# A fused attention, max-of-three and normalised-layer kernel: operand loads, weight pieces, rounding order and tile pairs rearranged

## The chip, the cores and the metric

One core of one Trainium2 chip runs the whole kernel in one launch. The metric is device time of one execution in microseconds (us), median of the runs shown.

## The reference, cut to what matters

```python
scores = q @ k.T / sqrt(64) - log(448)             # 4 batches x 12 heads x 448 x 64
x = (1 / (1 + exp(-scores))) @ v                   # -> x: 1792 tokens x 768
h = max(x @ w1, x @ w2, x @ w3) @ w_out            # 768 -> 768 -> 768, no nonlinearity after w_out
h = h @ w_in                                       # 768 -> 1024
e = exp(h - max(h)); solu = h * e / (sum(e) + 1e-9)
ln = (solu - mean(solu)) / sqrt(var(solu) + 1e-6) * g_ln
out = ln @ moe2_w_out                              # 1024 -> 768
```

## The kernel before, in words

Every matmul is done with operands cut into a high part (the value rounded to the format that TensorE takes) and a low part (the value minus its high part). Three matmuls stand for one: high-high, high-low, low-high. The high part is a cast on ScalarE (ACT), the low part a subtraction on VectorE (DVE). Large products are taken seven at a time (P1 to P7 in `PROD`) with sums of blocks as operands (A11, S1 to S4, ... on one side, B11, T1 to T4, ... on the other).

The stages, in the order in which TensorE (PE) does them:

- First half of attention, 0 to about 95 us of the span.
- `gen_w` (L462): the product of `w_out` and `moe2_w_in`, which replaces two layers by one weight. Its parts go to DRAM tensors `w_d`. Between its matmuls `run_bg` (L328) takes steps of a queue `bg` of generators; in it stand `prepare` (operands of this product, tiles `r_wo`) and `convert_w2` (L406: one of 16 blocks of the last weight, scaled by `g`, cut and written to DRAM `w2_d`; tiles `raw`, `w2s`). Before, one block of the 16 stands there, two more in the second half of attention (150 to 216 us).
- The layer of w1, w2, w3 ("first layer"; `product`, L632): 9 groups of weights, each used by two units of 63 matmuls (token halves). `convert_group` (L557) prepares the next group in `bg`, and the remaining 13 blocks of `convert_w2` lie in the groups as `LATE` (L34) says. `RATE` (L36) is the number of steps for each matmul. `sums` (L650) gathers the result in tiles `hs` and writes them to DRAM `h_d` (L672).
- The bridge: `load_wf` (L714) brings seven weights of 1.5 MB from `w_d` through POOL's queue as the memory of the first layer comes free; `load_h` (L691) brings the tokens' `h` back from `h_d`, 128 tokens to a tile `a`, through SP's queue.
- Seven units "L" (each a pair of 128-token tiles, 63 matmuls of 512 columns), numbered L0 to L6, and then seven units "O" (84 matmuls of 384 columns), O0 to O6. `product_c` (L842) does one product; `prep_l` (L750) and `prep_o` (L946) prepare the seven operands of the next unit (tiles `c_L_A`, `c_L_S`, `c_O_A`, `c_O_S`), `solu_ln` (L879) normalises a tile of 128 tokens, transposes it and writes it to `u_d`, and `load_u` (L922) loads it as operand `ut`.

In the last 14 units the order of ACT's and DVE's instructions is written out by a credit. `pace` (L834) adds 0.227 (L) or 0.174 (O) after each matmul and, while the credit is positive, takes a step in turn from `bg` (operands) and `lazy` (normalising); each step states its cost. Before a product, `product_c` forces steps of `bg` until its operand has been issued:

```python
while key not in cops:
    assert step(bg), key
```

All instructions of PE, ACT and DVE run in that written order, each engine in its own queue. A unit runs P1, then P4 and P3 of the unit before it (`close`, L1006), then P2, P6, P5, P7. ACT copies the accumulator `X` out after P1 (L1038), P6 (L1073) and P7 (L1079) before PE may add the next product to it; DVE adds after P2, P7 and in `close`.

Of the kernel before, what the change touches and what calls it, by code (L numbers as in the profile page):

```python
# [6 lines left out]
F32 = mybir.dt.float32  # L7
# [25 lines left out]
EARLY, SECOND = 1, 2  # L33
LATE = (0, 1, 1, 2, 2, 2, 2, 2, 1)  # L34
RING = 10
RATE = (0.46, 0.38, 0.38) + 5 * (0.49,) + (0.4,)  # L36
# [9 lines left out]
def sigmoid_attention_max_moe_solu_ln(tc, q, k, v, w123, wo, wi, w2, g, out):  # L46
# [53 lines left out]
    w_d = {nm: dram.tile([P, 3, 2, 512], F32, name=f"w_d{nm}") for nm in LOADS}  # L100
# [8 lines left out]
    w2_second = w2_keys[EARLY : EARLY + SECOND]  # L109
    w2_left = [w2_keys[EARLY + SECOND + sum(LATE[:n]) : EARLY + SECOND + sum(LATE[: n + 1])] for n in range(NG)]  # L110
    rest_wo = [("wo", fc, i) for fc in range(1, FC) for i in range(2)]
    early = list(w2_keys[:EARLY])
    mid = rest_wo[:6]
    for n in range(6, len(rest_wo), 2):
        mid += [early.pop(0)] if early else []
        mid += [rest_wo[n], rest_wo[n + 1]]
    mid += early
    stream += mid + w2_second
# [56 lines left out]
    def prepare(key, fine=False):  # L175
        y = wip.tile([P, HU], F32, tag="y", name="y_" + "_".join(map(str, key)), bufs=3)
# [211 lines left out]
    sp.dma_start(out=g_sb, in_=g)  # L388
    MID = NP // 2
# [11 lines left out]

    FIN = [(nm, i) for i in range(3) for nm in TS]
    state["home"] = lambda k, name: stp.tile([P, 2 * QU], F32, tag="stg", name=name, bufs=2)
    state["w2s"] = 0

    def convert_w2(key):  # L406
# [17 lines left out]
        for n, src in enumerate((y[:, QU:], z[:, :QU], z[:, QU:], y[:, :OU])):  # L424
# [11 lines left out]
            (sp if state["home"] else pool).dma_start(  # L436
# [4 lines left out]
    def staging(name):  # L441
        k = state["w2s"]
        state["w2s"] += 1
        if k % 2 == 0 or state["home"] is None:
            return stp.tile([P, 2 * QU], F32, tag="stg", name=name, bufs=2)
        return state["home"](k, name)
# [15 lines left out]
    def gen_w(fc, n):  # L462
# [23 lines left out]
        def put(nm, src):  # L486
            t = wsp.tile([P, 2, 512], F32R, tag="ws", name=f"ws{nm}_{c}", bufs=3)
            copy(act, t[:, 0], src)
            yield
            rest(dve, t[:, 1], src, t[:, 0])  # L490
            sp.dma_start(out=w_d[nm][:, c], in_=t.bitcast(F32))
            yield
# [14 lines left out]
        if fc == FC - 1 and n == 0:  # L507
            wts[4] = temp(4)
            copy(act, wts[4], ps)
            bg.appendleft(put("B21", wts[4]))  # L510
        elif n == 1:
            b21 = pws[fc][:, 0] if fc < FC - 1 else wts[4]
            wts[2] = temp(2)
            tt(wts[2], ps, wts[1], ALU.subtract)
            tt(wts[3], ps, wts[3], ALU.subtract)
            now(put("B22", ps))
            if fc < FC - 1:
                now(put("B21", b21))
            tt(wts[1], b21, wts[2], ALU.subtract)
            bg.extendleft(put(nm, wts[k]) for nm, k in (("T4", 1), ("T3", 3), ("T2", 2)))  # L520

    wts = {}
    bg.extend(prepare(key, True) if key[0] == "wo" else convert_w2(key) for key in mid)
# [14 lines left out]
    state["home"] = None  # L538
# [58 lines left out]

    tsplits = [split_t(0, nm, i) for nm in ("T1", "T4", "T3", "T2") for i in range(3)]
    bg.append(mix(run_steps(tsplits + [convert_group(0)]), run_steps(convert_w2(key) for key in w2_second)))


# [89 lines left out]
    def load_h(p, k):  # L691

        for i in range(2):
            t = tiles[2 * p + i]
            a = f_tile(*FIN[4 * (1 - p % 2) + i + 2 * k], f"a{p}_{i}{k}")[:, :HU]
            sp.dma_start(
                out=a.rearrange("p (f t) -> p f t", f=3),
                in_=h_d[k][:, :, t * P : (t + 1) * P].rearrange("f p t -> p f t"),
            )
            hts[(p, i, k)] = a  # L700
# [38 lines left out]
    def split_l(key, src):  # L739
        t = place(key)  # L740
        while t is None:
            yield None
            t = place(key)
        copy(act, t[:, 0], src)
        yield 0.05
        rest(dve, t[:, 1], src, t[:, 0])
        cops[key] = [t[:, m] for m in range(2)]
        yield 0.56

    def prep_l(p):  # L750
        a11, a12, a21, a22 = (hts.pop((p, i, k)) for i, k in ((0, 0), (0, 1), (1, 0), (1, 1)))
        yield from split_l(("L", p, "A11"), a11)
        yield from split_l(("L", p, "A12"), a12)
        s1 = f_tile(*FIN[8 + p % 2], f"s1_{p}")[:, :HU]
        tt(s1, a21, a22, ALU.add)
        yield 0.56
        tt(a21, a11, a21, ALU.subtract)
        yield 0.56
        tt(a11, s1, a11, ALU.subtract)
        yield 0.56  # L760
        yield from split_l(("L", p, "S2"), a11)
        yield from split_l(("L", p, "S1"), s1)
        yield from split_l(("L", p, "S3"), a21)
        yield from split_l(("L", p, "A22"), a22)
        tt(a12, a12, a11, ALU.subtract)
        yield 0.56
        yield from split_l(("L", p, "S4"), a12)
# [3 lines left out]
    for n, u in enumerate(units):  # L771
# [8 lines left out]
        if old is not None:  # L780
# [4 lines left out]
            if old["u"] == (NG - 1, 1):  # L785
# [6 lines left out]
                load_h(0, 1)  # L792
# [11 lines left out]
        if u == (NG - 1, 1):  # L804
            loads = pin(ET.Pool)
            shut(xd_cm)
            wslot.update(weight_slots("sa", (0, 1)))
            for tag in (0, 1):
                load_wf(LOADS[tag], tag)
            load_h(0, 0)  # L810
# [56 lines left out]
    def new_st(t):  # L867
        st = tp.tile([P, 12], F32, tag="st", name=f"st{t}", bufs=16)
        return [st[:, i : i + 1] for i in range(12)]

    h2s, sts, uts = {}, {}, {}

    def add_max(dst, ps, other, top):
# [274 lines left out]
```

## Time and profile before

| | us |
|---|---|
| median of 3 runs | 815.06 (809.72 to 815.38) |
| the profiled execution | 810.48 |
| its span in the profile | 808.7 |
| PE busy / DVE busy / ACT busy in it | 684.3 / 501.6 / 376.1 |

The rows below come from one profiled execution. [...] An instruction's idle time is that of its engine just before it, with what ended it.

### The profile page before, as it was taken

The page shows a single profiled execution, that of the slowest core. Times are in us where ns is not written, and L with a number is a line of the kernel's source. Part 1 is how long each engine was busy: PE and PEld are TensorE (multiplying, and loading weights), DVE is VectorE, ACT ScalarE, POOL GpSimd, SP SyncE. Part 2 cuts the span into 40 slices and gives each one's busy share as a digit, 9 for nine tenths or more (in the row PEclk, how much of TensorE's full clock was granted, in tenths as well). Part 3 has the DMA queues.
Part 4 walks back from the last instruction along what each step waited for, and adds up shares of the span by engine and source line. Part 5 has one row for each costly group of instructions (what it writes and reads, how often), then busy time and mean ns, then how long its engine had stood idle before and what let it go on. Part 6 is the DMA issues. An engine that isn't in the chain of part 4 may idle for free.

```text
span 808.7 us, 9695 instructions
## 1 busy us (share of the span) xinstructions
PE 684.3 (85%) x3283; PEld 543.8 (67%) x3283; DVE 501.6 (62%) x1140; ACT 376.1 (46%) x716; POOL 73.4 (9%) x128
## 2 busy tenths in 40 slices
PE   9999979899999999999998256977776677767677
PEld 6555856445599999999998245755554577656567
DVE  3999866787587776887783225754454645454524
ACT  6886324678654445455540113643342443434322
POOL 1111110021000111101101010000014200000000
PEclk9999989899999999999999587998999978998869
DMA  8787577556113565466627692222157922313131
GB/s 292 215 258 236 186 263 278 189 177 174 64 35 99 154 201 151 120 193 203 168 54 278 243 324 59 86 85 65 39 145 249 273 84 92 98 62 101 59 94 60
DMA packets 79234, 125.43 MB, mean 155 GB/s; under 512 B 31984, under 2 KB 60048, under 8 KB 78288
## 3 DMA queue, kind: packets, MB, share of 16 engines
q1 hardware_dynamic: 68144, 69.72, 27.4%
q0 software_dynamic: 10896, 54.86, 21.3%
q8 instruction: 26, 0.43, 0.2%
q10 hardware_dynamic: 144, 0.23, 0.1%
q14 instruction: 24, 0.20, 0.1%
HBM read 84.41 MB, written 40.37 MB: 154 GB/s over the span
## 4 chain that ended last, share of the span: by engine, by line
PE 63%; DVE 16%; ACT 9%; DMA 8%; issue 3%; SPq 0%; ACTq 0%; DVEq 0%
PE x L642 15%; PE X L852 15%; PE v L642 7%; PE av L279 7%; PE V L852 5%; PE sc L258 5%; PE z L642 4%; DMA h_d<-hs 3%; DMA a<-h_d 2%; PE sc L254 2%; PE Z L852 2%; DVE h L886 1%; ACT c_O_S L52 1%; DVE h L874 1%; DMA w_dB<-wsB 1%
## 5 line engine op out<-in xcount | busy, mean ns | idle before, releaser
L279 PE MATMUL av<-sf,vr 128*64 128x448 f32 x384 | 79.8, 559 | 0.0
L266 ACT ACTIVATE sf<-sc,bias_s 128x896 f32<-128x896 f32 x72 | 67.8, 1010 | 1.5
L475 PE MATMUL pw<-wi_t,r_wo 128*128 128x512 f32 x216 | 53.1, 407 | 7.1 <-DVE r_wo L54 7.1
L258 PE MATMUL sc<-qt,kt 64*128 64x448 f32 x432 | 51.9, 379 | 4.8 <-ACT sf L263 4.7
L852 PE MATMUL X<-wfT,c_L_S 128*128 128x512 f32 x126 | 33.8, 413 | 26.0 <-ACT h L1073 16.6
L279 PEld LDWEIGHTS av<-sf,vr 128*64 128x64 f32 x384 | 26.0, 140 | 42.8 <-issue 37.1
L475 PEld LDWEIGHTS pw<-wi_t,r_wo 128*128 128x128 f32 x216 | 42.2, 197 | 18.1 <-DVE r_wo L54 7.9
L852 PE MATMUL X<-w2tT,c_O_S 128*128 128x384 f32 x168 | 38.2, 374 | 15.0 <-ACT c_O_S L52 13.6
L642 PE MATMUL x<-T3h,S 128*128 128x448 f32 x108 | 34.9, 378 | 17.5 <-ACT u L682 17.5
L258 PEld LDWEIGHTS sc<-qt,kt 64*128 64x128 f32 x432 | 39.0, 186 | 15.8 <-ACT sf L263 6.2
L148 POOL DMA_DIRECT2D raw<-in_w x52 | 28.4, 546 | 226.4 <-DVE w2s L57 122.6
L852 PE MATMUL X<-w2tB,c_O_A 128*128 128x384 f32 x84 | 27.4, 493 | 25.2 <-ACT c_O_A L52 24.4
L852 PEld LDWEIGHTS X<-wfT,c_L_S 128*128 128x128 f32 x126 | 23.7, 196 | 34.9 <-ACT h L1073 17.4
L852 PEld LDWEIGHTS X<-w2tT,c_O_S 128*128 128x128 f32 x168 | 32.2, 209 | 19.5 <-ACT c_O_S L52 15.9
L57 DVE TENSOR_TENSOR c_L_A<-a,c_L_A 128x384 fp32r<-128x384 f32 x21 | 11.6, 554 | 51.6 <-ACT c_L_A L52 51.6
L852 PEld LDWEIGHTS X<-w2tB,c_O_A 128*128 128x128 f32 x84 | 21.8, 282 | 29.8 <-ACT c_O_A L52 26.7
L682 ACT COPY u<-x 128x448 f32<-128x448 f32 x36 | 19.1, 531 | 47.3 <-PE x L642 47.2
L642 PEld LDWEIGHTS x<-T3h,S 128*128 128x128 f32 x108 | 21.1, 195 | 19.6 <-ACT u L682 17.8
L642 PE MATMUL x<-B11h,A 128*128 128x448 f32 x108 | 33.7, 366 | 0.0
L642 PE MATMUL v<-T1h,S 128*128 128x448 f32 x108 | 33.6, 365 | 0.0
L642 PE MATMUL v<-B22h,S 128*128 128x448 f32 x108 | 33.6, 365 | 0.0
L642 PE MATMUL x<-T2h,S 128*128 128x448 f32 x108 | 33.6, 365 | 0.0
(183 smaller groups left out, 1635.8 us busy)
## 6 DMA issues: line engine op xcount, KB each, us to landing
raw<-in_w POOLq DMA_DIRECT2D x52, 384.0 KB, 4.1
w_d<-w2s SPq DMA_DIRECT2D x42, 192.0 KB, 2.4
u_d<-ub SPq DMA_DIRECT2D x14, 512.0 KB, 2.7
ut<-u_d SPq DMA_DIRECT2D x56, 128.0 KB, 3.4
kr<-in_k SPq DMA_DIRECT2D x24, 256.0 KB, 3.6
vr<-in_v SPq DMA_DIRECT2D x24, 256.0 KB, 3.8
raw<-in_wi POOLq DMA_DIRECT2D x16, 384.0 KB, 4.5
w_dT<-wsT SPq DMA_DIRECT2D x12, 512.0 KB, 3.5
```

The costliest lines, as they stand in the source:

```text
L52: act.copy(dst, src)
L57: eng.tensor_tensor(out=dst, in0=src, in1=hi.bitcast(F32), op=ALU.subtract)
L148: pool.dma_start(out=t, in_=source(key).rearrange("p (n t) -> p n t", t=2))
L254: pe.matmul(sc[:, 0, :S], lhsT=kt[:, x, c * P :], rhs=qt[:, y], start=start, stop=stop)
L258: pe.matmul(sc[:, j, :S], lhsT=kt[rows, x, c * P : (c + 1) * P], rhs=qt[rows, y], start=start, stop=stop)
L266: act.activation(sf, sc[:, :, :S], AF.Sigmoid, bias=bias_s, scale=1.0 / math.sqrt(D))
L279: pe.matmul(pa[j * D : (j + 1) * D, :S], lhsT=vr[:, j, c], rhs=sf if c == 3 else sf[:, j], start=(n == 0), stop=(n == 3),)
L475: pe.matmul(ps, lhsT=wt[:, a, cols], rhs=wi_t[:, b, c0 : c0 + 512], start=(i == 0), stop=(i == 3 * KC - 1))
L642: pe.matmul(ps, lhsT=l, rhs=r, start=(start and c == 0 and i == 0), stop=(stop and c == 2 and i == 2), skip_group_check=True)
L682: act.copy(e, ps)
L852: pe.matmul(ps, lhsT=hl[l][:, c * P : (c + 1) * P], rhs=wt[:, c, m], start=(start and c == 0 and i == 0), stop=(stop and c == chunks - 1 a ...
L874: dve.tensor_tensor_reduce(out=dst, in0=ps, in1=other, scale=1.0, scalar=-3.0e38, op0=ALU.add, op1=ALU.max, accum_out=top)
```

## The change

- `convert_w2` leaves the `gen_w` stage and the second half of attention: all 16 blocks lie in the first layer, two in each of groups 1 to 8. The rates of groups 1 and 2 rise to that of the others. `ws` gets four buffers, `y` two.
- The weights in `w_d` get a row pitch of 528 instead of 512 numbers, so that a load of 1.5 MB consists of pieces of 2 KB instead of 12 KB.
- The first pair's `h` gets tiles of its own. Its first two thirds are loaded before the last sums, and its last third straight from `hs`.
- `prep` replaces `split_l` and `split_o`: the cast of the next operand is issued before the subtraction of the last, in 12 steps instead of 18. It is queued after P6 instead of before P2 (L) and after P2 (O).
- `load_u` stands before P2 instead of after it, and waits until the pair after it has been normalised too. `load_w2` for the last layer's first weight moves by one unit.
- `solu_ln` works on a pair of tiles: sign and 1/1024 are folded into other instructions, the one-column instructions work on two columns, and the transposed tile takes the memory of `e`.

```diff
-LATE = (0, 1, 1, 2, 2, 2, 2, 2, 1)
+LATE = (0,) + 8 * (2,)
-RATE = (0.46, 0.38, 0.38) + 5 * (0.49,) + (0.4,)
+RATE = (0.46,) + 7 * (0.49,) + (0.4,)
...
-    w_d = {nm: dram.tile([P, 3, 2, 512], F32, name=f"w_d{nm}") for nm in LOADS}
+    w_d = {nm: dram.tile([P, 3, 2, 528], F32, name=f"w_d{nm}") for nm in LOADS}
...
-    bg.extend(prepare(key, True) if key[0] == "wo" else convert_w2(key) for key in mid)
+    bg.extend(prepare(key, True) for key in rest_wo)
...
+    def last_rows(k):
+        for i in range(2):
+            t = tiles[i]
+            b, c0 = divmod(t * P, S)
+            sp.dma_start(out=hts[(0, i, k)][:, 2 * P :], in_=hs[(k, b)][:, c0 : c0 + P])
...
-        pool.dma_start(out=t.bitcast(F32), in_=w_d[nm])
+        pool.dma_start(out=t.bitcast(F32), in_=w_d[nm][:, :, :, :512])
...
+    def prep(kind, p, a11, a12, a21, a22, s1, view, cost):
+        ready = {}
+        def high(nm, src):
+            parts = halves_of((kind, p, nm))
+            while parts is None:
+                yield None
+                parts = halves_of((kind, p, nm))
+            ready[nm] = (src, parts)
+            copy(act, view(parts[0]), src)
+        def low(nm):
+            src, parts = ready.pop(nm)
+            rest(dve, view(parts[1]), src, view(parts[0]))
+            cops[(kind, p, nm)] = parts
+        yield from high("A11", a11)
+        yield 0.1
+        yield from high("A12", a12)
+        low("A11")
+        yield cost
+        tt(s1, a21, a22, ALU.add)
+        yield cost
+        low("A12")
+        yield cost
+        tt(a21, a11, a21, ALU.subtract)
+        yield cost
+        tt(a11, s1, a11, ALU.subtract)
+        yield cost
+        yield from high("S2", a11)
+        tt(a12, a12, a11, ALU.subtract)
+        yield cost
+        yield from high("S1", s1)
+        low("S2")
+        yield cost
+        yield from high("S3", a21)
+        low("S1")
+        yield cost
...
     def load_u(p):
         for t in tiles[2 * p : 2 * p + 2]:
-            while t not in turned:
+            while t not in turned or (p + 1 < NP2 and tiles[2 * p + 3] not in turned and p > 0):
                 assert step(lazy), t
...
         if n + 1 < NP2:
             load_h(p + 1, 0)
             load_h(p + 1, 1)
-            bg.append(prep_l(p + 1))
+        elif n + 1 < len(stage):
+            load_u(n + 1 - NP2)
...
-        if NP2 - 1 <= n < len(stage) - 1:
-            load_u(n + 1 - NP2)
-            bg.append(prep_o(n + 1 - NP2))
         product_c(X, kind, p, "P6", False, False)
         release(kind, p, "P6")
+        if n + 1 < NP2:
+            bg.append(prep_l(p + 1))
+        elif n + 1 < len(stage):
+            bg.append(prep_o(n + 1 - NP2))
```

The steps of `solu_ln` cost 0.2, 1.6, 0.3, 0.2, 0.7 and 1.25 for each tile before, 8.5 in 12 steps for a pair, and 7.64 in 13 steps after. `prep` costs 0.56 (L) or 0.69 (O) in each of 11 steps and 0.1 in one; before, an operand took 0.05 and 0.56 or 0.69 in two steps, and each of the four sums as much in one.

## Rows read from the trace of the kernel before

**Rows 1.** Stages of core 0: length, each engine's busy time and instructions, PEclk, DMA.

```profile
105.00:150.00 45.00, 35.12 (x153) 25.10 (x153) 28.50 (x58) 19.31 (x33) 2.69 (x5) 0.88 0.73 257
150.00:216.00 66.00, 63.97 (x384) 32.81 (x382) 47.43 (x108) 50.84 (x82) 9.13 (x14) 0.98 0.51 152
...
293.00:420.00 127.00, 127.00 (x628) 117.69 (x627) 99.80 (x238) 65.99 (x159) 14.04 (x26) 1.00 0.55 158
...
442.00:492.00 50.00, 16.56 (x67) 13.69 (x66) 12.93 (x25) 7.84 (x16) 3.21 (x6) 0.72 0.70 262
...
509.00:623.00 114.00, 84.35 (x319) 62.53 (x317) 60.81 (x166) 47.63 (x92) 9.99 (x14) 0.93 0.36 110
623.00:783.00 160.00, 116.28 (x498) 103.00 (x498) 77.26 (x172) 60.03 (x113) 7.13 (x10) 0.85 0.37 115
```

**Rows 2.** TensorE's timeline, 85 to 225: start, length, operation, count, idle before.

```profile
116.42 13.29 PE L475 MATMUL pw<-wi_t,r_wo 128*128 128x512 f32 x45 [5.93 <-DVE r_wo L54]
...
146.96 1.49 PE L258 MATMUL sc<-qt,kt 64*128 64x448 f32 x6 [2.78 <-ACT sf L263]
...
182.02 0.86 PE L258 MATMUL sc<-qt,kt 64*128 64x448 f32 x6 [1.89 <-ACT sf L263]
```

**Rows 3.** ScalarE's timeline, 88 to 118 us.

```profile
110.61 0.54 ACT L52 CAST w2s<-raw 128x192 fp32r<-128x192 f32 x2 [4.53 <-DMA w_d<-w2s]
```

**Rows 4.** TensorE's timeline, the bridge.

```profile
459.93 0.74 PE L642 MATMUL x<-T3h,S 128*128 128x448 f32 x1 [17.46 <-ACT u L682]
...
491.64 3.65 PE L852 MATMUL X<-wfT,c_L_S 128*128 128x512 f32 x9 [15.98 <-ACT h L1073]
```

**Rows 5.** ScalarE's timeline, the same stretch.

```profile
458.93 0.51 ACT L52 CAST c_L_A<-a 128x384 fp32r<-128x384 f32 x1 [24.60 <-DMA a<-h_d]
...
487.26 0.51 ACT L52 CAST c_L_A<-a 128x384 fp32r<-128x384 f32 x1 [17.31 <-DMA a<-h_d]
```

**Rows 6.** POOL's queue, 405 to 500 us.

```profile
431.93 1.08 POOL L716 DMA_DIRECT2D wfB<-w_dB  x2 [19.92 <-DMA a<-h_d]
```

**Rows 7.** DMA queues, 438 to 442 us: packets, MB, share of 16 engines.

```profile
q0 software_dynamic: 134, 1.49, 87.4%
q1 hardware_dynamic: 123, 0.20, 13.0%
```

**Rows 8.** DMA issues, 442 to 446 us: KB each, median us to landing.

```profile
h_d<-hs SPq DMA_DIRECT2D x2, 224.0 KB, 12.9
```

**Rows 9.** DMA queues, 612 to 616 us.

```profile
q0 software_dynamic: 336, 1.18, 89.4%
```

**Rows 10.** TensorE's timeline, first products of L1, L2 and O0.

```profile
495.13 2.20 PE L852 MATMUL X<-wfB,c_L_A 128*128 128x512 f32 x9
...
509.41 2.20 PE L852 MATMUL X<-wfB,c_L_A 128*128 128x512 f32 x9
...
622.98 3.88 PE L852 MATMUL X<-w2tB,c_O_A 128*128 128x384 f32 x12 [2.94 <-ACT c_O_A L52]
```

**Rows 11.** TensorE's timeline, waits of O3, first products of O3, O4, O6.

```profile
698.28 0.62 PE L852 MATMUL X<-w2tB,c_O_A 128*128 128x384 f32 x2 [3.94 <-ACT c_O_A L52]
...
710.83 2.73 PE L852 MATMUL X<-w2tT,c_O_S 128*128 128x384 f32 x12 [1.90 <-ACT c_O_S L52]
714.65 2.74 PE L852 MATMUL V<-w2tT,c_O_S 128*128 128x384 f32 x12 [1.09 <-ACT c_O_S L52]
...
723.55 3.84 PE L852 MATMUL X<-w2tB,c_O_A 128*128 128x384 f32 x12 [4.08 <-ACT c_O_A L52]
...
783.22 0.62 PE L852 MATMUL X<-w2tB,c_O_A 128*128 128x384 f32 x2 [3.58 <-ACT c_O_A L52]
```

**Rows 12.** Groups by line and form, 510 to 809 us, VectorE and ScalarE.

```profile
L57 DVE TENSOR_TENSOR c_O_A<-ut,c_O_A 128x512 fp32r<-128x512 f32 x21 | 14.4, 687 | 29.7 <-ACT c_O_A L52 29.7
...
L60 DVE TENSOR_TENSOR u<-V,u 128x384 f32<-128x384 f32 x14 | 7.8, 557 | 30.0 <-ACT u L1079 18.7 <-PE V L852 11.2
...
L1079 ACT COPY u<-X 128x384 f32<-128x384 f32 x7 | 3.3, 469 | 16.6 <-PE X L852 16.6
```

More of the change, by code (lines that the diff above doesn't have):

```diff
@@ L737, in place, with halves_of @@
         return ring.tile([P, 2, HU], F32R, tag="ring", name="c_" + "_".join(map(str, key)))
[L739 to L742, printed above, removed]
+    def halves_of(key):
+        if key[0] == "L":
             t = place(key)
[L744 to L748, printed above, removed]
+            return t if t is None else [t[:, m] for m in range(2)]
+        if not clear(state["ops"] - RING) or not clear(state["ops"] + 1 - RING):
+            return None
+        return [place(key).rearrange("p a b -> p (a b)")[:, :512] for m in range(2)]
@@ new lines, in prep @@
+    def prep(kind, p, a11, a12, a21, a22, s1, view, cost):
[33 more added lines that the diff above has]
+        yield cost
+        yield from high("A22", a22)
+        low("S3")
+        yield cost
+        yield from high("S4", a12)
+        low("A22")
+        yield cost
+        low("S4")
+        yield cost
@@ L865, in charge, with new_st, add_min @@
         credit["t"] -= cost
-    def new_st(t):
-        st = tp.tile([P, 12], F32, tag="st", name=f"st{t}", bufs=16)
-        return [st[:, i : i + 1] for i in range(12)]
     h2s, sts, uts = {}, {}, {}
-    def add_max(dst, ps, other, top):
+    turned = set()
+    def new_st(p):
+        st = tp.tile([P, 9, 2], F32, tag="st", name=f"st{p}", bufs=8)
+        sts[p] = [st[:, i] for i in range(9)]
+        return sts[p]
+    def add_min(dst, ps, other, low, first):
         dve.tensor_tensor_reduce(
-            out=dst, in0=ps, in1=other, scale=1.0, scalar=-3.0e38, op0=ALU.add, op1=ALU.max, accum_out=top
+            out=dst, in0=ps, in1=other, scale=-1.0, scalar=first, op0=ALU.add, op1=ALU.min, accum_out=low
@@ L1012, in close @@
         if kind == "L":
+            first, low = (x[:, 1:] for x in sts[p][:2])
             dve.tensor_scalar(
-                out=cx, in0=o["X"], scalar1=1.0, scalar2=None, op0=ALU.mult, op1=ALU.max, accum_out=o["top"][3]
+                out=cx, in0=o["X"], scalar1=-1.0, scalar2=first, op0=ALU.mult, op1=ALU.min, accum_out=low
             )
-            charge(0.85)
+            charge(0.78)
         else:
@@ L1022, in close @@
         if kind == "L":
-            add_max(u2, o["V"], u2, o["top"][1])
-            lazy.append(both(*(solu_ln(t) for t in tiles[2 * p : 2 * p + 2])))
+            first, low = (x[:, :1] for x in sts[p][:2])
+            add_min(u2, o["V"], u2, low, first)
+            lazy.append(solu_ln(p))
         else:
```

221 lines of the change are left out of this document (91 added, 130 removed).

## The prediction

> **What bounds the kernel now.** I read the stages first, then what TensorE waited for in each, then what stood ahead of that work in the other engines' queues. In the stages [rows 1] look at the first number after the length: from 293 to 420 us PE is busy all 127 us, so nothing done there for the other engines can show. It has no work in 9.9 of 45 us (105 to 150), 33.4 of 50 (442 to 492), 29.7 of 114 (509 to 623) and 43.7 of 160 (623 to 783). In none of these is DVE or ACT full: in the last stage they are busy 48% and 38%. So the last two stages are bound by the order of three in-order queues that wait for each other, not by an engine.
>
> The bridge has two holes, 17.46 and 15.98 us [rows 4]. PE's releaser there is ACT copying an accumulator; ACT itself had sat before an earlier instruction of its queue, a cast whose source `a` came by DMA, for 24.60 and 17.31 us [rows 5]. So the accumulator copy was stuck behind a late load. What made the load late: POOL started the weight loads at 431.93 [rows 6], and in the 4 us that follow 438 the software queue moved 134 packets of 1.49 MB (11 to 12 KB each) while SP's queue moved 123 packets of 0.20 MB [rows 7]. The two queues take turns packet by packet, so a small row pays for a 12 KB piece. A write of 224 KB took 12.9 us there [rows 8].
>
> Where one product follows another without a wait, an L unit takes 509.41 - 495.13 = 14.28 us for 63 matmuls, 0.227 each [rows 10]; that was L1, with the queue of normalising only beginning to fill. Later units are slower: L2 to O0 took 622.98 - 509.41 = 113.6 us for five units, and O3 723.55 - 698.28 = 25.3 us [rows 10, 11]. In O3 PE waits 1.90 us before P6, 1.09 before P5 and 4.08 before the next P1, 7.1 in all [rows 11]; 84 matmuls at the pace of 0.174 that `pace` assumes are 14.6 us, which leaves 3.6 for the granted clock, 0.85 on average in this stage [rows 1].
>
> **Blocks of the last weight.** One block leaves `gen_w`. ACT stood there 4.53 us for a DMA out of `w2s` [rows 3]; the operand cast behind it reached PE 5.93 us late, and the 45 matmuls after that took 13.29 us where 45 x 0.227 = 10.2 [rows 2]. Both go: 5.93 + 3.1 = 9.0. The waits at 146.96 and 182.02, 2.78 and 1.89 us [rows 2], are on ACT too; the second has the other two blocks beside it, of the first I cannot say what share is theirs. I take 11 of 13.7; between 4 (DVE, busy 63% there, is next late) and 14. The three blocks go to groups 1 and 2 and the last group. Their cover is a full PE: with two blocks in each group DVE is busy 99.8 of 127 us and PE never waits [rows 1]. A block is some nine DVE instructions; at 99.8 / 238 = 0.42 us each, 3.8 us, so three cost nothing there, and at most 11 if that cover failed. In the last group, 28 steps at 0.4 a matmul are 70 of its 126 matmuls, done before the bridge. Their writes join SP's queue ahead of the first `h` loads, which then have about 10 us until they are needed.
>
> **The bridge.** P7 of the last first-layer unit could have run at 459.93 - 17.46 = 442.5 [rows 4]. From there: P7 1.8 us, P1 of L0 2.0, the two left products 3.7, the other four of L0 8.2, all of L1 14.3: P1 of L2 at 472.5 instead of 509.41, 36.9 us earlier, if nothing waits. The first pair's operands no longer stand behind the weights: two thirds of each are loaded before, and the last third is a quarter of a megabyte in all, out of memory on the core. The second pair's load still follows the last writes of `h`, since it takes the memory of `hs`; I leave 1.5 us for it. What is late next is the weights, 11.0 MB in seven loads through one queue from 431.93. In 12 KB pieces they move at 1.49 MB in 87.4% of 4 us, 426 GB/s [rows 7]. No row shows 2 KB pieces of this queue; the nearest are its 3.5 KB packets, 1.18 MB in 89.4% of 4 us, 330 GB/s [rows 9], and as the average of those 4 us 295. I take 330. Then the first five (7.86 MB) are there at 456, when P7 of L0 wants the fifth, and the seventh at 466, when P3 of L0 wants it at 462: about 4 late. 36.9 - 1.5 - 4.4 = 31. At 426 the wait is gone (37); at 250, a guess below the last average for 2 KB and for the operand loads' turns, the seventh comes at 476, which leaves 20.
>
> [...]
>
> **The last twelve units.** The cause of their waits is the lead with which operands are issued. Before, the operands of an O unit are 18 steps (7 x 0.74 + 4 x 0.69 = 7.9) and the normalising of a pair 12 steps (8.5). A unit's credit is 14.6 less three charges of 0.56, 12.9. As the two queues take turns, 12.9 / (0.44 + 0.71) = 11 steps of each are taken: 7 of the 18 are left until a product forces them, that is, until they stand in ACT's and DVE's queues behind the copy and the sum that wait for PE's last product. Every operand is then a round trip. After: 12 steps of 0.64 against 13 of 0.59, so 12.9 / 1.23 = 10.5 of 12 are taken in time, and only one or two are forced. By the same sum an L unit goes from 10 of 18 to 10 of 12. By the order of the steps, those forced are the low parts of A11 (for P1) and of S2 (for P6); S1 for P5 comes ahead of the copy, so its 1.09 goes. What a forced P1 still waits for: the copy after P7, 0.47, the sum, 0.56, and one subtraction, 0.69 [rows 12], with hand-overs 1.9, less the two matmuls that need no low part, 0.35: 1.6. P6 likewise, with a sum of two operands in the place of the copy, 1.6. An O unit is then 14.6 + 3.2 + 1.7 for the clock (half of before's 3.6, as half of the waits are left) = 19.5; an L unit, with a shorter subtraction and a longer sum, 14.3 + 2.8 + 1.4 = 18.5. The normalising is paced to end at about O4 (`load_u` forces it there); O5 without it I put at 16, and O6 with the end at 24 instead of 808.7 - 783.22 = 25.5 [rows 11]. Sum 5 x 18.5 + 5 x 19.5 + 16 + 24 = 230 us instead of 808.7 - 509.41 = 299.3: 69 less. Bounds: 30 (rival two) and 105 (rival one).
>
> What these edits add: `load_u` now waits for one more normalised pair, and forces its steps ahead of P2; its eight DMAs go out ahead of the write of `e`. With `ub` in the memory of `e`, the second exponential of the next pair waits for a DMA out of the tile three back; behind it on ACT stand the casts and copies. In the credit's order the transpose lies some 4 us ahead of it, about the time of that write, so I put it at nothing, with one or two us for each of seven pairs as the worst. The 14 or so one-column instructions that fall away for each pair are taken from a DVE that is 48% busy: nothing by themselves.
>
> **Sum.** The profiled execution took 810.48 (span 808.7 and 1.8 around it): 810.5 - 11 - 31 - 69 = 699.5. The median of the runs stands 0.6% above that execution; half of that makes 701.
>
> **Rivals.** One, the lead suffices (chance 0.13): with integer steps nothing is forced, waits vanish as in L1. Twelve units at 15.3 to 16 and the end at 23 make 194, 105 less, and the whole 664. For it: L1 at 14.28 [rows 10]. Against: 10.5 is below 12. Two, ACT takes the place of the forced steps (0.2): its exponentials, squares and scalings wait for DVE in the middle of the queue, and copies stand behind them. Then little but the wait before P5 and some clock comes back, 30 us, and the whole is 738. For it: ACT already sits 30 us before DVE's sums can run [rows 12]. Three, a piece is not a turn (0.1): the operand loads stay at about 10 us in the bridge, and the second hole stays for the most part; 16 instead of 31 and the whole about 715. Against it: the one-to-one packets [rows 7]. [...] Four, slower (0.05): the 2 KB pieces cost POOL's software queue time for each piece. Seven loads have six times the pieces. The forecast turns into a loss when the seventh load lands 115 us later than 466, at 581: 21 us a load instead of 4. At six times the present pace, 3.7 us for 1.57 MB at 426 GB/s, it is 22 us a load and the whole about 820. Against it: the pieces of 3.5 KB already run at 330 [rows 9].
>
> **How the numbers follow.** The forecast, 701, has 0.52. From 670 to 742 lie it, the third and nearly all of the second; left out are most of the first and the fourth. Faster by over 1% (about what this kernel's runs can tell from no change) 0.95, within 1% 0.01, slower 0.04.
>
> **What would show it.** In the profile after: no hole above 3 us between 442 and 480 less 11; SP's packets landing in 3 to 4 us beside the weights; no r_wo wait of 6 us in `gen_w`; PE full through the first layer; O units of 19 to 20 us with no wait before P5 and waits of 1.5 to 2 before P1 and P6. It is wrong if the units still take 23 us and more, if ACT sits before `e` or `h` while PE waits for a copy, or if weights arrive after their products.

## The result, and the profile after

The changed kernel takes 713.25 us (median of 4 runs, 712.01 to 716.61); the kernel before, timed beside it, 813.49. The ratio is 0.8779, 95% interval 0.8732 to 0.8827. The forecast was 701. The profiled execution took 716.61 (the slowest of the four), its span 714.8 against 808.7: 93.9 us less, which I split where the prediction did; by the medians it is 100.2. The medians here and below leave out one slow execution, of 720.56 us, in one of the experiments.

The stages of the changed kernel (columns as in [rows 1]; times from the span's start, PEclk the clock granted to TensorE as a share of full speed). The whole first layer is one row, since the three blocks went to groups outside of 293 to 420. 430 to 488 goes from P7 of the last first-layer unit to P1 of L2 (442 to 509 before), 488 to 571 is L2 to L6 (509 to 623 before), 571 to 623 is O0 and O1, 623 to 715 is O2 to the end:

```profile
105.00:150.00 45.00, 41.51 (x215) 28.07 (x213) 34.09 (x67) 22.29 (x35) 1.61 (x3) 1.00 0.76 263
...
205.37:430.12 224.75, 224.75 (x1109) 207.74 (x1107) 174.78 (x407) 113.64 (x272) 24.86 (x45) 1.00 0.53 154
...
430.00:488.00 58.00, 37.64 (x135) 30.15 (x135) 22.49 (x45) 16.35 (x32) 6.34 (x9) 0.76 0.75 254
488.00:571.00 83.00, 76.19 (x320) 58.86 (x318) 61.55 (x142) 51.58 (x100) 5.70 (x8) 1.00 0.39 120
571.00:623.00 52.00, 39.23 (x164) 32.90 (x162) 24.34 (x45) 18.30 (x35) 11.41 (x16) 0.84 0.77 227
623.00:715.00 92.00, 82.15 (x444) 79.55 (x442) 51.86 (x92) 40.12 (x77) 0.00 (x0) 0.96 0.35 113
```

Look at PE's number and at the clock behind the POOL column. From 105 to 150 PE is busy 41.5 us instead of 35.1; the first layer is full with the three blocks in it and takes 224.8 us, where it took 224.6 before (217.85 to 442.47); five L units have few holes and the full clock. Two stages are still bad: 430 to 488 (37.6 busy of 58, clock 0.76) and 571 to 623 (39.2 of 52, clock 0.84).

**Until the bridge.** P7 of the last first-layer unit could have run at 441.76 - 11.64 = 430.1 instead of 442.5: 12.4 us gained, 11 forecast. By the end of `gen_w` 9.5 us have come back (132.39 instead of 141.87), and 3.0 more by the start of the first layer (205.37 instead of 217.85). The page's group of `gen_w`, the one that the 5.93 us wait belonged to [rows 2], has no idle time left:

```profile
L469 PE MATMUL pw<-wi_t,r_wo 128*128 128x512 f32 x216 | 49.6, 390 | 0.0
```

**The bridge**, 430.1 to P1 of L2: 58.3 us instead of 66.9, so 8.6 gained where 31 were forecast. TensorE's timeline (start, length, operation, count, idle before), ScalarE's, and POOL's queue:

```profile
441.76 0.74 PE L638 MATMUL x<-T3h,S 128*128 128x448 f32 x1 [11.64 <-ACT u L678]
...
461.79 4.18 PE L894 MATMUL X<-wfT,c_L_S 128*128 128x512 f32 x9 [3.48 <-DMA wfT<-w_dT]
...
474.11 4.05 PE L894 MATMUL X<-wfT,c_L_A 128*128 128x512 f32 x9 [5.24 <-ACT h L1095]
...
488.45 2.26 PE L894 MATMUL X<-wfB,c_L_A 128*128 128x512 f32 x9
```

```profile
429.76 0.51 ACT L51 CAST c_L_A<-a 128x384 fp32r<-128x384 f32 x1 [8.19 <-DMA a<-hs]
...
469.76 0.51 ACT L51 CAST c_L_A<-a 128x384 fp32r<-128x384 f32 x1 [12.50 <-DMA a<-h_d]
```

```profile
419.77 0.85 POOL L724 DMA_DIRECT2D wfB<-w_dB  x1 [15.05 <-PE x L638]
428.29 0.84 POOL L724 DMA_DIRECT2D wfB<-w_dB  x1 [7.67 <-issue]
437.48 0.84 POOL L724 DMA_DIRECT2D wfT<-w_dT  x1 [8.35 <-issue]
```

Three holes of 20.4 us together are left of 33.4 [rows 4]. The first and the third are of the kind of before: an accumulator copy on ACT stands behind a cast whose source is still on its way (the third now stands before P4 of L0, no longer before P7). The second is new: a weight is late. POOL's rows say why: one load of 1.5 MB stood in the queue at a time, and the next was issued 7.8 to 9.2 us later, up to the seventh at 469.80. "issue" means that POOL waited for nothing that the profile shows. Before, two loads were issued back to back [rows 6]. The unhindered bridge was 30 us in the prediction; 58.3 - 30 - 20.4 = 8 us beside the holes are for the most part the lower clock: behind a hole the nine matmuls of a product take 3.1 to 4.2 us (445.28, 461.79, 474.11; granted clock 0.69, 0.50 and 0.52), at the full clock 2.26 (488.45).

**The last twelve units**, P1 of L2 to the end: 226.35 us instead of 299.3, 72.9 gained, 69 forecast. The stretch before and after (columns as in [rows 1]):

```profile
509.41:808.70 299.29, 221.34 (x922) 185.36 (x920) 147.65 (x351) 113.45 (x216) 17.12 (x24) 0.89 0.35 107
...
488.45:714.80 226.35, 197.11 (x922) 170.95 (x920) 137.65 (x277) 109.67 (x208) 17.11 (x24) 0.95 0.46 142
```

So 48.7 us of the 72.9 are idle time of PE that went (78.0 to 29.2), and 24.2 are the same 922 matmuls taking less time at a higher granted clock (0.95 instead of 0.89). TensorE's timeline, waits of O1, O2, O3 and O4 and the first products of O3 and O5:

```profile
608.95 1.33 PE L894 MATMUL V<-w2tB,c_O_S 128*128 128x384 f32 x3 [1.91 <-DMA w2tB<-w_d]
...
622.61 0.62 PE L894 MATMUL X<-w2tB,c_O_A 128*128 128x384 f32 x2 [1.09 <-ACT c_O_A L51]
623.88 3.01 PE L894 MATMUL X<-w2tB,c_O_A 128*128 128x384 f32 x10 [0.66 <-DVE c_O_A L56]
...
641.09 2.75 PE L894 MATMUL X<-w2tB,c_O_A 128*128 128x384 f32 x12 [1.08 <-ACT c_O_A L51]
...
651.41 2.00 PE L894 MATMUL X<-w2tT,c_O_S 128*128 128x384 f32 x10 [0.88 <-DVE c_O_S L56]
...
661.25 2.82 PE L894 MATMUL X<-w2tB,c_O_A 128*128 128x384 f32 x10 [2.08 <-DVE c_O_A L56]
...
677.17 2.25 PE L894 MATMUL X<-w2tB,c_O_A 128*128 128x384 f32 x12
```

O2 waits 1.75 us before and inside P1, O3 1.08 before P1 and 0.88 inside P6, O4 0.97 + 2.08 = 3.05 before and inside P1; nothing waits before P5. Before the change O3 waited 1.90 before P6 and 1.09 before P5, and the P1 behind it 4.08 [rows 11]. O2 to O4 take 18.5, 17.5 and 18.6 us, O5 and O6's first part 14.6 each. But O0 takes 25.0 and O1 27.0: there PE waits for `w2tT` and `w2tB`, the last layer's weights, 8.4 us in all. Together they take 51.9 us where they took 51.1 before (622.98 to 674.12): these two units gained nothing.

### The profile page after: what moved, and what is told of

It is laid out like the page before. It is cut to its first block, busy times and chain, and to the rows that moved or that the text cites. A ratio compares the mean times of both kernels' runs of the same rounds, so it can differ in the third digit from the quotient of the medians.

```text
span 714.8 us, 9650 instructions
## 1 busy us (share of the span) xinstructions
PE 659.2 (92%) x3283; PEld 529.2 (74%) x3283; DVE 489.8 (69%) x1057; ACT 372.4 (52%) x709; POOL 69.3 (10%) x121
## 4 chain that ended last, share of the span: by engine, by line
PE 66%; DVE 12%; DMA 8%; issue 7%; ACT 4%; POOL 2%; SPq 0%; DVEq 0%; ACTq 0%; POOLq 0%
PE x L638 18%; PE X L894 12%; PE v L638 8%; PE av L271 7%; PE V L894 6%; PE z L638 4%; PE sc L250 4%; PE Z L894 3%; DMA h_d<-hs 3%; PE sc L246 2%; POOL w2tT L730 2%; DMA a<-h_d 1%; DMA a<-hs 1%; DVE y_wo L156 1%; DVE wt L59 1%
## 5 line engine op out<-in xcount | busy, mean ns | idle before, releaser
L271 PE MATMUL av<-sf,vr 128*64 128x448 f32 x384 | 77.5, 545 | 0.0
L469 PE MATMUL pw<-wi_t,r_wo 128*128 128x512 f32 x216 | 49.6, 390 | 0.0
L469 PEld LDWEIGHTS pw<-wi_t,r_wo 128*128 128x128 f32 x216 | 40.4, 188 | 9.3 <-issue 1.0
L638 PE MATMUL x<-T3h,S 128*128 128x448 f32 x108 | 35.0, 379 | 11.6 <-ACT u L678 11.6
L894 PE MATMUL X<-w2tT,c_O_S 128*128 128x384 f32 x168 | 34.7, 351 | 6.5 <-DMA w2tT<-w_d 3.6
L894 PEld LDWEIGHTS X<-w2tT,c_O_S 128*128 128x128 f32 x168 | 29.8, 194 | 9.5 <-DVE c_O_S L56 3.2
L59 DVE TENSOR_TENSOR u<-V,u 128x384 f32<-128x384 f32 x14 | 7.8, 558 | 39.5 <-PE V L894 19.8
L894 PEld LDWEIGHTS X<-wfT,c_L_S 128*128 128x128 f32 x126 | 24.5, 197 | 12.9 <-issue 3.9
L638 PE MATMUL x<-T4h,A 128*128 128x448 f32 x108 | 33.6, 365 | 0.0
L638 PE MATMUL z<-B21h,A 128*128 128x448 f32 x108 | 33.6, 365 | 0.0
L638 PEld LDWEIGHTS x<-T3h,S 128*128 128x128 f32 x108 | 21.1, 195 | 14.0 <-ACT u L678 12.2
## 6 DMA issues: line engine op xcount, KB each, us to landing
kr<-in_k SPq DMA_DIRECT2D x24, 256.0 KB, 3.3
vr<-in_v SPq DMA_DIRECT2D x24, 256.0 KB, 3.7
```

The source lines that it names most:

```text
L59: dve.tensor_tensor(out=dst, in0=a, in1=b, op=op)
L271: pe.matmul(pa[j * D : (j + 1) * D, :S], lhsT=vr[:, j, c], rhs=sf if c == 3 else sf[:, j], start=(n == 0), stop=(n == 3),)
L469: pe.matmul(ps, lhsT=wt[:, a, cols], rhs=wi_t[:, b, c0 : c0 + 512], start=(i == 0), stop=(i == 3 * KC - 1))
L638: pe.matmul(ps, lhsT=l, rhs=r, start=(start and c == 0 and i == 0), stop=(stop and c == 2 and i == 2), skip_group_check=True)
L894: pe.matmul(ps, lhsT=hl[l][:, c * P : (c + 1) * P], rhs=wt[:, c, m], start=(start and c == 0 and i == 0), stop=(stop and c == chunks - 1 a ...
```

## The experiments

Each was timed beside the kernel before, whose medians there were 809.65 to 813.76; so a difference of a few us between two experiments may be one between those occasions. Times are medians of 4 runs, where nothing else is said; "the changed kernel" is 713.25. Theory A of the first four: the bridge is bound by the weights, of which one at a time stands in the queue. Theory B: piece size is innocent, the order of the operand loads makes the bridge.

**Pieces of 12 KB again.**

```diff
-    w_d = {nm: dram.tile([P, 3, 2, 528], F32, name=f"w_d{nm}") for nm in LOADS}
+    w_d = {nm: dram.tile([P, 3, 2, 512], F32, name=f"w_d{nm}") for nm in LOADS}
```

> The changed kernel with the 2 KB pieces undone: the weight loads of the bridge are one 12 KB piece a partition again. Theory A (the bridge of the changed kernel is bound by its weights: a load of 768 pieces is issued only when the last has landed, so that one goes out every 8.3 us): POOL issues the loads without waiting for each other, one lands about every 4 us, and PE waits for no weight; the operand loads pay for 12 KB turns again, so the hole before P7 of the last first-layer unit grows from 11.6 us to 15 to 19 us. Both together about nothing: 705 to 720 us. Theory B (the pieces are innocent of the late weights and only help the operand loads): weights as late as in the changed kernel, operand loads later, 725 to 735 us.

721.33 us (718.85 to 724.83), ratio 0.8876 (0.8820 to 0.8932), just above the range of theory A. POOL's queue:

```profile
418.12 1.07 POOL L724 DMA_DIRECT2D wfB<-w_dB  x2 [14.86 <-PE x L638]
423.60 1.60 POOL L724 DMA_DIRECT2D wfT<-w_dT  x3 [4.40 <-PE v L638]
```

Five loads stand in the queue within 7 us, none waits; the instruction takes 0.53 us instead of 0.84. The weights are no longer late, but the operands are: the holes are 21.19 us before P7 (15 to 19 expected) and 9.98 before P4 of L0, and P1 of L2 comes at 495.18. So the small pieces are worth 8 us, nearly all that the bridge gained. DMA queues of this kernel, 434 to 438 us (packets, MB, share of 16 engines):

```profile
q0 software_dynamic: 146, 1.59, 93.0%
q1 hardware_dynamic: 146, 0.07, 5.7%
```

One packet to one in these 4 us, of 10.9 KB and 0.5 KB on average; with 4 KB pieces it is 361 to 362, of 3.9 and 0.6 KB (below). A packet is one piece of 12 or of 4 KB, but two of 2 KB: from 428.29 to 437.48 the changed kernel moves one load of 768 pieces, 1.57 MB, in 400 packets.

**Pieces of 4 KB; the first pair's operands queued later; both.** In the second edit `prep_l(0)` enters `bg` after the accumulator copies of the last first-layer unit.

```diff
-    w_d = {nm: dram.tile([P, 3, 2, 528], F32, name=f"w_d{nm}") for nm in LOADS}
+    w_d = {nm: dram.tile([P, 3, 1040], F32, name=f"w_d{nm}") for nm in LOADS}
```

```diff
                 last_rows(1)
-                bg.append(prep_l(0))
...
+        if n == len(units) - 1:
+            bg.append(prep_l(0))
         old = dict(u=u, X=X, V=V, u2=u2)
```

> The changed kernel with pieces of 4 KB, 384 to a load instead of 768. Theory A: two loads find room, POOL's waits of 7 to 8 us go, the third to seventh weight lands 4 to 5 us after the one before it; the waits for weights in L0 (3.5 us, then 5.2 us behind a late operand) go, the hole before P7 stays at 10 to 13 us: 700 to 707 us. Theory B: nothing changes but a slower turn for the operand loads: 713 to 717 us.

> The changed kernel with one move: the operands of L0 are queued after the last first-layer unit's own copies instead of before them. The hole of 11.6 us before P7 should go in any case. Theory A: PE then runs into the weights, the third of which lands at about 445 us, and gains at most 3 us: 710 to 714 us. Theory B: operand order alone makes the bridge, and 9 to 11 us come back: 702 to 705 us.

> Both moves, 4 KB pieces and the operands of L0 queued late. Theory A: they only pay together, since each alone runs into the other: 690 to 698 us. Theory B: as with the late queueing alone, 702 to 705 us.

4 KB pieces: 720.71 us (717.78 to 722.06), a miss of both theories. POOL issues two loads together and the next three after waits of 6.9, 3.5 and 4.7 us, no product of L0 waits for a weight, but the load of the first pair's last third takes 12.2 us instead of 6.3 and the hole before P7 grows from 11.64 to 18.24. A turn is no longer than in the changed kernel, a packet of 4 KB in both; what differs is that the weights' queue has more under way (1.44 MB in 368 packets from 434 to 438, 0.72 in 191 in the changed kernel). Against 12 KB pieces SP's queue moves 372 packets instead of 146 in these 4 us, but the bridge is only 3 us shorter (63.3, 66.5) and the whole the same. So most of the 8 us that the small pieces gained are not the shorter turn; they came with the pauses of the weights' queue. Queued later: 713.53 (713.08 to 716.58), as A said: the hole before P7 is gone, P1 of L0 runs at 432.89 instead of 445.28, and then PE waits 2.69, 5.79 and 3.65 us for weights. Both: 710.16 (three runs, 709.91 to 717.39), where A said 690 to 698. No weight is late and P7 doesn't wait, but in TensorE's and ScalarE's timelines of this kernel stand these two rows:

```profile
471.87 3.65 PE L895 MATMUL X<-wfT,c_L_A 128*128 128x512 f32 x9 [13.56 <-ACT h L1096]
```

```profile
464.86 0.51 ACT L51 CAST c_L_A<-a 128x384 fp32r<-128x384 f32 x1 [9.54 <-DMA a<-h_d]
```

The late source is the second pair's load, which takes the memory of `hs` and so stands behind the last writes of `h`. Neither A nor B holds. The new theory: three things are late one behind another, and removing one uncovers the next.

**The second pair's load early, too.**

```diff
-            t = f_tile(*FIN[i + 2 * k], f"a{p}_{i}{k}")[:, :HU]
+            t = f_tile(*FIN[i + 2 * k + (4 if p == 1 else 0)], f"a{p}_{i}{k}")[:, :HU]
...
         if n == len(units) - 1:
             bg.append(prep_l(0))
+            load_h(1, 0)
+            load_h(1, 1)
```

> The 4 KB pieces and the late queueing of the first pair's operands as in the run with both, and in addition the second pair's h is loaded at the end of the last first-layer unit, into tiles whose memory is not that of the last hs tiles, so that its load no longer waits behind the last writes of h. Theory A (three things are late one behind another in the bridge: ACT's casts of the first pair, the weights, the second pair's load): the wait of P4 of L0 (13.56 us in the run with both) falls under 4, P1 of L2 comes at 470 to 477 instead of 485.8, and the whole is 698 to 704. Rival (the DMA queues carry a fixed amount of bytes between 415 and 470 and whatever is moved ahead makes the rest late): P1 of L2 stays at 482 to 488, the whole 709 to 715.

694.29 us (693.34 to 700.07), ratio 0.8586 (0.8529 to 0.8642), 4 below the expected range. TensorE's timeline, the first products of L0 and L2 and the one wait between; then the DMA queues, 434 to 438 us:

```profile
435.39 4.21 PE L897 MATMUL X<-wfB,c_L_A 128*128 128x512 f32 x9 [4.42 <-ACT c_L_A L51]
...
457.41 3.91 PE L897 MATMUL X<-wfT,c_L_A 128*128 128x512 f32 x9 [2.97 <-ACT h L1100]
...
471.63 2.26 PE L897 MATMUL X<-wfB,c_L_A 128*128 128x512 f32 x9
```

```profile
q0 software_dynamic: 361, 1.41, 85.9%
q1 hardware_dynamic: 362, 0.23, 17.8%
```

P1 of L2 comes 16.8 us earlier than in the changed kernel and the whole is 19.0 us shorter (15.7 by the ratios): the three causes are shown. The first two gain at most 3 us, alone or together; the third was run only together with both, so what it would give by itself is not shown. The rival, a fixed amount of bytes, falls: the same bytes pass sooner.

**Operands in 18 steps; low part directly behind its high part.** The first adds six empty steps and changes no instruction's place within the operand sequence; the second has each subtraction behind its own cast, in 11 steps of the same total cost (not 12, as the expectation says).

```diff
         yield from high("A11", a11)
-        yield 0.1
+        yield 0.05
         yield from high("A12", a12)
+        yield 0.05
         low("A11")
```

```diff
         yield from high("A11", a11)
-        yield 0.1
+        low("A11")
+        yield cost + 0.1
         yield from high("A12", a12)
-        low("A11")
+        low("A12")
         yield cost
```

> The operands of a unit in 18 steps again, by six additional empty steps of 0.05; order of the instructions, their costs and everything else as in the changed kernel. Theory of the prediction (the lead by number of steps is what the last twelve units gained): about 11 of 18 are taken in time, 7 are forced, the waits before P6 and P5 return, and the last twelve units, 226 us in the changed kernel, take 255 to 290; the whole 742 to 775. Rival (the cast ahead of the subtraction is what gained, not the number of steps): the whole 710 to 720.

> The 12 steps are kept, but each low part (subtraction) is issued directly behind its own high part (cast), as before the change, so that DVE waits for ACT's cast at every operand. Theory of the prediction (number of steps): within some 8 us of the changed kernel, 713 to 721, as only the order inside a step is another. Rival (the pipelined order is what gained): waits of 1 to 2 us before P6 and P5 of each unit, 20 to 50 us more, 733 to 763.

18 steps: 733.32 us (726.44 to 736.44), 20 more, which lies between the two expectations and meets neither; the last twelve units take 239.8 us. PE's waits for operands from 490 us (in total, times, longest), of this kernel and of the changed one:

```profile
PE X L900 <- DVE c_O_S L56: 5.8, 4, 2.1
...
PE X L900 <- DVE c_L_S L56: 4.9, 4, 1.4
...
PE X L900 <- ACT c_O_S L51: 2.7, 3, 1.9
```

```profile
PE X L894 <- DVE c_O_S L56: 2.2, 3, 0.9
PE X L894 <- DVE c_L_S L56: 2.1, 2, 1.3
PE X L894 <- ACT c_O_S L51: 0.7, 1, 0.7
```

The waits before P6 come back, 13.4 instead of 5.0 us; none before P5 (V) does. So the number of steps counts, as the prediction said, with a smaller price and without its wait before P5. Unpipelined: 721.28 (718.71 to 722.91), 8 more, just above the first expectation; the last twelve units take 231.4. Steps and order together are 18.5 us of the 72.9 by these spans (13.4 and 5.1; the second has one step fewer, so the order by itself may cost more). Something else gained more.

**Normalising tile by tile; operands queued as before; single columns in pair order.** The first takes each tile through exponential, product, square, scalar chain and transpose by itself, two tiles in turn, as before the change. The second puts `prep_l` before P2, `load_u` and `prep_o` after P2. The third keeps the pair's steps and only does the one-column instructions for each tile.

```diff
...
-        for i in range(2):
-            c = slice(i, i + 1)
-            act.activation(e[i], h[i], AF.Square, bias=su[:, c], scale=-float(F2), accum_out=vs[:, c])
-            yield 0.2
-        act.activation(z, ssum, AF.Square, bias=eps_z, scale=1e-3)
-        yield 0.2
+        act.activation(e, h, AF.Square, bias=su, scale=-float(F2), accum_out=vs)
+        act.activation(z, ssum, AF.Square, bias=eps_z, scale=1e-3)
+        yield 1.6
...
```

```diff
...
             load_h(p + 1, 1)
-        elif n + 1 < len(stage):
-            load_u(n + 1 - NP2)
+            bg.append(prep_l(p + 1))
...
```

```diff
...
-        tt(s1, s0, z, ALU.mult)
-        tt(s1, s1, s0, ALU.mult)
...
+        for c in cs:
+            tt(s1[:, c], s0[:, c], z[:, c], ALU.mult)
+            tt(s1[:, c], s1[:, c], s0[:, c], ALU.mult)
...
```

> The normalising works on one tile of 128 tokens at a time again, two tiles taken in turn, five steps for each (0.2, 1.6, 0.3, 0.8, 1.25) and one-column instructions; its arithmetic, and all else, as in the changed kernel. Order of operands and number of steps account for some 20 and 8 of the 73 us of the last twelve units by the two runs on them. Theory N (most of the rest is the normalising by pairs, since with single tiles ACT's exponential, square and scaling each wait for DVE with copies queued behind): 30 to 45 us more than the changed kernel, 743 to 760. Theory P (most of the rest is where the operands are queued and the tokens loaded): 713 to 725.

> The operands of the next unit are queued before P2 (L) and after P2 (O) as before the change, and the normalised tokens are loaded after P2, without the wait for one more pair; all else as in the changed kernel. Theory P (most of the rest is where the operands are queued and the tokens loaded): 30 to 45 us more, 743 to 760, in the O units above all. Theory N (it is the normalising by pairs): 710 to 722. By the prediction's credit, which counts a whole unit, the place matters little: 713 to 720.

> The normalising keeps the order and the steps of a pair, and only its one-column instructions are done tile by tile again (ten more on VectorE and three more on ScalarE for each pair). Theory A (what the pairs gained is the order: each large ScalarE instruction has the other tile's between it and the VectorE instruction that it needs): 713 to 721, of the 35 us that single tiles cost at most a fifth. Theory B (it is the fewer one-column instructions, whose chain of round trips is gone through once instead of twice): 735 to 750.

Tile by tile: 748.21 us (745.94 to 751.53), 35 more than the changed kernel; the last twelve units take 256.0, 30 more. ScalarE's waits for VectorE in them (total, times, longest): before the change, in this run, and in the changed kernel:

```profile
ACT e L888 <- DVE st L887: 16.1, 10, 3.8
ACT h L901 <- DVE st L900: 13.8, 10, 2.3
...
ACT st L894 <- DVE st L893: 8.4, 7, 2.0
```

```profile
ACT h L944 <- DVE st L943: 19.0, 9, 8.9
...
ACT e L932 <- DVE h L929: 11.7, 8, 2.6
```

```profile
ACT h L958 <- DVE st L954: 3.4, 5, 1.0
```

The square (L888, in this run L932) needs DVE's product of the same tile; the scaling (L901, L944, L958) needs DVE's chain of one-column instructions. With single tiles ACT stands before them in the middle of its queue, 31 us in all, and casts stand behind: PE's waits in the last twelve units that a cast ended are 30.2 us instead of 9.5, those that a subtraction ended 8.0 instead of 7.2. In pairs the other tile's large instruction lies between. In pair order with single columns: 718.48 (716.04 to 719.43), the last twelve units 225.1: it is not the smaller number of one-column instructions. A rival to the order is left: single tiles also make ten steps of 0.83 of thirteen of 0.59, and by the prediction's own sum 12.9 / (0.64 + 0.83) = 8.8 instead of 10.5 operand steps are then taken in time. Against it as the main cause: with 18 steps, where 11 of 18 are taken, the waits that grew most were those that a subtraction ended (14.3 us). What share of the 30 us it has was not tested. Queued as before: 720.00 (716.90 to 720.72). Its last twelve units take 222.2, no more than the changed kernel's; what it loses lies in the bridge, where the second pair's casts stand ahead of the accumulator copy of L0. TensorE's timeline and ScalarE's:

```profile
474.14 4.21 PE L894 MATMUL X<-wfT,c_L_S 128*128 128x512 f32 x9 [17.57 <-ACT h L1087]
```

```profile
470.08 0.51 ACT L51 CAST c_L_A<-a 128x384 fp32r<-128x384 f32 x1 [20.98 <-DMA a<-h_d]
```

**The last layer's weight in pieces of 3 KB.** High and low half of a row lie side by side in `w2_d`.

```diff
-    w2_d = [dram.tile([4, P, 2 * len(nms), HU], F32, name=f"w2_d{n}") for n, nms in enumerate(PIECES)]
+    w2_d = [dram.tile([4, P, len(nms), 2, HU], F32, name=f"w2_d{n}") for n, nms in enumerate(PIECES)]
...
-            pool.dma_start(out=t[:, kc].bitcast(F32), in_=w2_d[n][kc][:, off::w])
+            pool.dma_start(out=t[:, kc].bitcast(F32), in_=w2_d[n][kc][:, off])
```

> The two halves of each row of the last layer's weight lie side by side in DRAM, so that its 28 loads consist of 128 pieces of 3 KB instead of 256 of 1.5 KB; the writes become two for each. Else the changed kernel. Theory: O0 and O1 (24.96 and 26.97 us against 18 of the next ones) are bound by the number of pieces of the software queue, which holds one to two loads of 384 KB; with half the pieces the last weight arrives 8 to 12 us earlier, O0 and O1 lose 8 to 14 us together, the whole 699 to 706. Rival (they are bound by bytes: the rate of some 275 GB/s at 90 to 100% of the DMA engines stays): the whole 711 to 716.

702.13 us (700.68 to 702.71), ratio 0.8665 (0.8619 to 0.8711), as expected. (Of the 28 loads, 24 change; the four of the first weight were in 128 pieces of 3 KB before.) O0 and O1 take 18.2 and 21.4 us instead of 25.0 and 27.0. POOL's queue in the changed kernel and in this one:

```profile
557.22 2.13 POOL L730 DMA_DIRECT2D w2tB<-w_d  x3 [78.10 <-PE X L894]
561.14 0.73 POOL L730 DMA_DIRECT2D w2tB<-w_d  x1 [1.79 <-issue]
```

```profile
562.54 1.09 POOL L732 DMA_DIRECT2D w2tT<-w_d  x2 [4.20 <-PE Z L896]
563.91 2.81 POOL L732 DMA_DIRECT2D w2tT<-w_d  x5 [0.27 <-issue]
568.23 0.54 POOL L732 DMA_DIRECT2D w2tT<-w_d  x1 [1.52 <-DMA w2tT<-w_d]
```

Three loads of 256 pieces are issued before the fourth waits, and seven of 128. From 575 to 585 the DMA engines are nearly full in both, but carry 342 GB/s here and 282 in the changed kernel: the software queue's packets take 64.1% of the engines for 1.83 MB there, 83.8% for 2.88 MB here. So in these two units the limit is the engines' time, which larger pieces use better; the theory's room in the queue need not have mattered.

**Both improvements in one kernel**, the early second pair and the 3 KB pieces:

> The run with the second pair's load early (4 KB pieces, operands queued late, other memory) and the run with 3 KB pieces of the last layer's weight in one kernel. The two act in different stages, so the gains should add: 694.3 - 11 = 683, within 680 to 688; if the earlier end of the bridge makes the weights of the last layer late again by as much, 690 to 695.

688.25 us (686.79 to 690.85), ratio 0.8465 (0.8430 to 0.8500), just above the expected 680 to 688: the fastest version, 25 us under the changed kernel. The second edit adds 6 to the first by the medians, 11 were expected; by the profiled executions it is 11.6 (700.07, that kernel's slowest, and 688.45), by the ratios 9.8, and O0 and O1 take 18.2 and 21.7 instead of 25.5 and 26.7, so the gain is there, with its size uncertain between 6 and 12.

## Why the prediction was right, and where it was not

The forecast of 701 is 12 us below the median, well inside 670 to 742. By the terms of its sum, on the profiled executions:

| term | forecast | measured |
|---|---|---|
| blocks leave `gen_w` | 11 | 12.4 |
| bridge | 31 | 8.6 |
| last twelve units | 69 | 72.9 |

**Blocks.** Right: no idle time is left in the group of `gen_w`, which with the slow matmuls behind it gave 9.5 us (9.0 forecast), and three blocks in the first layer cost nothing under its full PE. The other 2 us, 3.0 measured, came in another way than forecast: the waits of the second half of attention are 4.2 us in five places (2.08 at 143.71 is the largest) instead of 4.7 in two, but the clock granted there is 1.00 instead of 0.96, and PE is busy 68.8 us instead of 71.2. Only the trace says this; the blocks were not put back.

**Bridge.** The step that failed is the rate, "I take 330", GB/s, with 250 as the low end: it lets the seven loads follow one another without a gap. 2 KB pieces gave seven loads of 1.57 MB in about 58 us (419.77 to the landing of the last, issued at 469.80 and some 8 us on its way), 190 GB/s. While a load moves, its pieces are not slow; between loads the queue stands empty for a time. The software queue of the changed kernel from 454 to 456 us, between two loads, and from 457 to 459, within one:

```profile
q0 software_dynamic: 19, 0.08, 25.7%
...
q0 software_dynamic: 191, 0.78, 98.6%
```

Rival four had looked at the right queue and at its number of pieces, but what it named was time for each piece; its threshold was 21 us a load, and it was 8.3 instead of 3.7. It was put aside with pieces of 3.5 KB that run at 330 [rows 9], and that reading was wrong: these are packets, and the loads in them had pieces of 1.5 KB (24 loads of 256 pieces make 2,688 packets from 600 to 660 us). Secondly, the prediction asked what is late next only once, and answered "the weights". By the experiments three things were: casts in ACT's queue ahead of the copy that PE waits for, the weights, the second pair's load behind the writes of `h`. For the third I had left 1.5 us; once the others are gone its hole is 13.56 us, and P1 of L2 comes 14.2 us earlier with the load moved (485.82 to 471.63). That a piece of 12 KB is a turn was right, packets went one to one (134 to 123 before, 146 to 146 with 12 KB again). That the turn is what makes the loads late was right only in small part: with 4 KB pieces the holes of 18.24 and 10.47 us stay for the most part, which is what rival three expected of them, for another reason. Writes of 224 KB took 6.5 us beside the weights (median of eight from 410 to 470; 6.4 before from 410 to 500, of which [rows 8] shows two that took 12.9), not the 3 to 4 forecast; and weights that arrive after their products, by the prediction's own signs a mark of being wrong, are what L0 shows.

**Last twelve units.** The sum was right, its composition was not, and that the parts cancel is luck: L2 to L6 and O2 to O4 came out 14 us below the forecast, O0 and O1 13 above. L2 to L6 took 82.2 us (92.5 forecast), O0 and O1 51.9 (39), O2 to O4 54.6 (58.5), O5 14.6 (16), O6 with the end 23.1 (24). The prediction put all 69 us on the lead of the operands. The fewer one-column instructions it put at nothing, which the run in pair order bears out; that a pair's order takes ACT's waits away had no term. Undone alone, steps cost 13.4 us of span, the unpipelined order 5.1, single tiles 29.7; queueing as before none. That is 48 of 72.9 (63 by the medians, which take in the bridge); the rest must lie in edits that were not undone or in their acting together, and stays open. The waits of ACT for DVE by which rival two would have spoilt the gain were already there before the change, 38 us of them, and the pairs removed them. (The row given for that rival says something else: the 30 us in [rows 12] are DVE's idle time before its sums, 18.7 of them ended by ACT's copy.) What was left for a forced operand was sized about right: 1.6 forecast for P1, 1.08 to 3.05 in O2 to O4, where the cast of A11 is late and not only its low part; 1.6 for P6, 0.88 in O3 and none in O2 and O4; none for P5. The stall of O0 and O1 was in no step: the first of these 24 loads is issued 13.5 us before P1 of O0 instead of 20.6 before the change, and they go out over 46 us instead of 35 (557.22 to 603.29; 602.39 to 637.61), beside more bytes of SP's queue (4.52 MB from 555 to 610; 3.76 from 600 to 660 before). That pieces of 3 KB end most of it is shown; how much the shorter L units have to do with it is not.

## What to carry to other kernels

When a hole closes, list everything that is due in it before costing the gain: three late arrivals in one place gave 8.6 of the 31 us forecast until all three were moved, and then 16 to 19 more. In an in-order queue, an instruction that needs another engine's answer wants independent work of the same size between, here the other tile's (its 30 us include what the other step sizes cost), and a cast that waits for a transfer belongs behind the copies that others wait for. The size of a transfer's pieces is a compromise: large ones made the other queue's rows wait their turn (in 4 us 146 of its packets passed beside pieces of 12 KB, 372 beside 4 KB), small ones filled the software queue (one load of 768 pieces at a time, 7.8 to 9.2 us apart), and a queue that was not empty held up the other's loads at 4 KB as well (12.2 us instead of 6.3).

## What the runs showed of the hardware

POOL's queue stopped by number of pieces, not by loads or bytes. The weight loads of the bridge have 1.57 MB each. Five of them in 128 pieces each were issued without waiting for the queue (12 KB pieces, 418.12 and 423.60); in 768 pieces the second waited 7.67 us behind the first (428.29). Loads issued before the next waited: seven of 128 (896 pieces; 1.52 us at 568.23 with 3 KB pieces), three of 256 (768; 1.79 us at 561.14), two of 384 (768; 6.93 us at 426.93 with 4 KB pieces), one of 768. The next one would have made 1,024 pieces or more in each case where it waited. Mixed loads agree: at 469.80 and 470.62 the changed kernel issues 768 and 128 pieces back to back, and the next 128 wait 6.31 us. Room for at least 896 and fewer than 1,024 pieces fits all of these; that is an estimate from these rows. What sets the room, no run shows. The issuing instruction took longer with more pieces, too: 0.53 to 0.60 us for 128, 0.71 for 256, 0.76 for 384, 0.84 for 768.
